# Two attention blocks on one core: exponentials without a shift, a range check with a second program behind a branch, and another split of the PSUM banks

## The chip, the cores and the metric

The kernel runs on one core of a Trainium2 chip. The metric is device time in microseconds (us). TensorE is called PE (its weight loads PEld), ScalarE ACT, VectorE DVE, GpSimd POOL and the engine that issues the DMAs SP. Every run is one of a program on one core.

## The reference, cut to what matters

Two blocks whose outputs stand side by side, each with 2048 rows, width 1024 and 32 heads of width 32.

```python
# A: full attention
scores = einsum('bhqd,bhkd->bhqk', q, k) * Dh ** (-0.5)      # 2048 x 2048 per head
p = softmax(scores); o = einsum('bhqk,bhkd->bhqd', p, v);  out_A = o @ wo
# B: four segments of 512 rows; causal softmax inside one, plus a memory of the earlier ones
p = softmax(logits + mask); a_dot = p @ vs
a_mem = (pq @ M) / (pq @ z + 1e-6);  o = g * a_mem + (1 - g) * a_dot
M = M + pk^T vs;  z = z + sum(pk);   out_B = o @ wo
```

A softmax stays the same if the exponent is shifted by any number per row. Without a shift it is right as long as no exponential overflows and no sum vanishes; with these inputs the scores are small.

## The kernel before: the parts that the change touches

The kernel is a list scheduler in Python. It keeps a model of each engine's time, records instructions in an order that this model likes, and writes that fixed order out with semaphores, so the order is settled before the kernel runs.

```python
SLOTS = [(0, 1, 2), (3, 4)]      # PSUM banks of the two score slots
OLB = 5                          # PV output and row sums
PROJ = [6, 7]                    # "side" work: projections, norms, memory, output projection
RING = 20                        # 512-column places for exponentials in SBUF
...
def emit_scores(self, it, n, banks):          # n = 3 or 2 heads of one item
    for part in range(2):                     # two matmuls of 256 columns a bank;
        for bk, (u, st, h) in zip(banks, todo):      # heads sit on different 32-row groups of PE
            ... mms.append((self.ps[:, bk, off:off + w], lhsT, rhs))
    R.op("PE", f, ..., mode="R")
    ...
    cb = self.cbA[b][:, k:k + 1]              # shift: one column, from norms of Q and K
    R.op("ACT", lambda e: e.activation(self.PT[:, s0:s0 + n, 0:width],
             self.ps[:, banks[0]:banks[0] + n, 0:width], ACTF.Exp, bias=cb, scale=SCALE), ...,
         cost=0.171 + n * width * 0.000833)
...
def a_norm(...):     # squares on DVE, column sums on PE, then maxima, a diagonal and a broadcast
...
# in the scheduler's loop, when PE would idle early on: keep it busy with a dummy matmul
if now < 45 and ... and gap >= 0.3 and bank is not None:      # bank: a free one of PROJ + [OLB]
    R.op("PE", lambda e, bank=bank: e.matmul(self.ps[:, bank, :], self.PT[:, RING - 1, 0:P], ...))
```

PE does three kinds of work in turn: scores (row groups), PV with its row sums (column groups), and side work on the whole array.

## Time and profile before

| kernel before | value |
|---|---|
| median of 4 runs | 1350.14 us (1347.47 to 1351.28) |
| PE, ACT busy | 91%, 89% of the span |
| exponentials of scores | 832 (A) + 160 (B) |
| start to start of two exponentials, back to back (median in the trace) | 1424 ns at 1536 columns, 997 ns at 1024: 143 ns + 0.834 ns a column |

The page of the kernel before: busy time, slices of ACT and of the granted PE clock, the chain that ended last, and the two groups of exponentials. A digit stands for a fortieth of the span, and 9 means 90% or more. The chain is followed back from the last instruction to what released each step; a name with q is an engine's sequencer, and "issue" is time with no wait that the profile shows.

```profile
PE 1232.8 (91%) x16968; PEld 509.2 (38%) x17194; DVE 831.7 (62%) x1391; ACT 1206.6 (89%) x1037; POOL 113.9 (8%) x207
...
ACT  3358989999999999999999999999999999999811
...
PEclk9889999999999998999999999999998999999998
...
ACT 66%; PE 23%; DVE 5%; SPq 2%; DMA 2%; issue 1%; POOL 0%; DVEq 0%
...
L471 ACT ACTIVATE PT<-ps,cbA 128x1024 bf16<-128x1024 f32 (+1 forms) x832 | 1013.1, 1365 | 25.1 <-PE ps L454 24.6
...
L471 ACT ACTIVATE PT<-ps,cbB 128x768 bf16<-128x768 f32 (+3 forms) x160 | 171.4, 1197 | 62.5 <-PE ps L454 61.5
```

ACT is full except for the first four slices and the last three, and it holds 66% of the chain. That looks like one bound. But PE has hardly more room, which its busy share does not tell and the order of its weight loads does. Below is the timeline of the kernel before on PEld (start, us, line, how many, idle time before in brackets):

```profile
604.46 0.12 PEld L454 LDWEIGHTS ps<-QA,KA 32*128 32x128 bf16 x6 [0.42 <-ACT PT L471]
604.78 0.10 PEld L520 LDWEIGHTS ps<-PT,VA 128*32 128x32 bf16 x4 [0.21 <-issue]
...
605.33 0.11 PEld L454 LDWEIGHTS ps<-QA,KA 32*128 32x128 bf16 x4 [0.21 <-ACT PT L471]
605.65 0.33 PEld L594 LDWEIGHTS ps<-xA,WA 128*128 128x128 bf16 x3 [0.21 <-issue]
```

Six score matmuls take 604.78 - 604.46 = 0.32 us to the next kind, and four take the same: the heads of one part run side by side, so two or three concurrent heads cost the same. Of the 0.32 us about 0.11 is the change of kind: the two parts of 256 columns take 0.21, since 512 columns of a projection start every 0.215 us in the same trace. The Trainium skill names a cause ("TensorEngine Tiling (Array Packing)", Tiling Modes, Key Properties: changing the tiling mode drains the engine); the gap of 0.21 us before the first load of the next kind, which the loads within one PV run do not have, agrees. Adding up such runs from 200 to 1200 us left PE some 50 us in 1000. That is my estimate, which no view shows; the windows view has PE busy for 929.5 of these 1000 us, with matmul ends that are modelled.

### The profile page before, as it was taken

The page shows a single profiled execution, that of the slowest core. Times are in us where ns is not written, and L with a number is a line of the kernel's source. Part 1 is how long each engine was busy: PE and PEld are TensorE (multiplying, and loading weights), DVE is VectorE, ACT ScalarE, POOL GpSimd, SP SyncE. Part 2 cuts the span into 40 slices and gives each one's busy share as a digit, 9 for nine tenths or more (in the row PEclk, how much of TensorE's full clock was granted, in tenths as well). Part 3 has the DMA queues.
Part 4 walks back from the last instruction along what each step waited for, and adds up shares of the span by engine and source line. Part 5 has one row for each costly group of instructions (what it writes and reads, how often), then busy time and mean ns, then how long its engine had stood idle before and what let it go on. Part 6 is the DMA issues. An engine that isn't in the chain of part 4 may idle for free.

```text
span 1350.1 us, 37376 instructions
## 1 busy us (share of the span) xinstructions
PE 1232.8 (91%) x16968; PEld 509.2 (38%) x17194; DVE 831.7 (62%) x1391; ACT 1206.6 (89%) x1037; POOL 113.9 (8%) x207
## 2 busy tenths in 40 slices
PE   6788999999999988999899999999998999999996
PEld 3433343333333333333333333333333333333442
DVE  3665456555675567656647754757566675567674
ACT  3358989999999999999999999999999999999811
POOL 1000000100011011101100010111011111011110
PEclk9889999999999998999999999999998999999998
DMA  7325122311211122112211112111210113111111
GB/s 211 63 59 130 25 41 62 74 37 25 64 37 33 21 56 37 29 29 60 49 40 30 33 25 58 31 37 30 49 32 21 37 29 96 44 30 43 53 59 47
DMA packets 195870, 66.39 MB, mean 49 GB/s; under 512 B 187008, under 2 KB 187008, under 8 KB 195712
## 3 DMA queue, kind: packets, MB, share of 16 engines
q1 hardware_dynamic: 195712, 63.99, 20.2%
q8 instruction: 135, 2.21, 0.7%
q14 instruction: 23, 0.19, 0.0%
HBM read 40.90 MB, written 8.39 MB: 37 GB/s over the span
## 4 chain that ended last, share of the span: by engine, by line
ACT 66%; PE 23%; DVE 5%; SPq 2%; DMA 2%; issue 1%; POOL 0%; DVEq 0%
ACT PT L471 65%; PE ps L594 13%; PE ps L454 5%; PE ps L520 5%; DVE OL L540 2%; SPq L335 2%; ACT E L762 1%; DVE OL L530 1%; DMA PKt<-PH 1%; DVE outsb L837 1%; DMA WB<-in_B_wk_dram 0%; DMA out_dram<-outsb 0%; SPq L305 0%; DVE SQB L604 0%; DVE KQB L604 0%
## 5 line engine op out<-in xcount | busy, mean ns | idle before, releaser
L471 ACT ACTIVATE PT<-ps,cbA 128x1024 bf16<-128x1024 f32 (+1 forms) x832 | 1013.1, 1365 | 25.1 <-PE ps L454 24.6
L454 PE MATMUL ps<-QA,KA 32*128 32x256 bf16 x4096 | 328.7, 275 | 32.3 <-ACT PT L471 21.0
L520 PE MATMUL ps<-PT,ones 128*32 128x256 bf16 (+1 forms) x4864 | 315.0, 274 | 0.0
L520 PE MATMUL ps<-PT,VA 128*32 128x256 bf16 x4096 | 274.7, 282 | 1.5 <-DVE OL L530 0.8
L540 DVE RECIPROCAL OL<-OL 128x128 f32<-128x128 f32 x256 | 242.3, 948 | 5.2
L471 ACT ACTIVATE PT<-ps,cbB 128x768 bf16<-128x768 f32 (+3 forms) x160 | 171.4, 1197 | 62.5 <-PE ps L454 61.5
L454 PEld LDWEIGHTS ps<-QA,KA 32*128 32x128 bf16 x4096 | 95.3, 92 | 302.3 <-ACT PT L471 249.9
L594 PE MATMUL ps<-xB,WB 128*128 128x512 bf16 x683 | 187.2, 393 | 23.6 <-issue 13.2
L594 PE MATMUL ps<-xA,WA 128*128 128x512 bf16 x679 | 181.0, 385 | 14.1 <-issue 12.7
L491 POOL TENSOR_SCALAR_AFFINE_SELECT PT<-PT 128x512 bf16<-128x512 bf16 (+2 forms) x143 | 83.8, 601 | 1097.7 <-ACT PT L471 1096.5
L520 PEld LDWEIGHTS ps<-PT,VA 128*32 128x32 bf16 x4096 | 107.9, 95 | 134.3 <-issue 125.7
L530 DVE COPY OL<-ps 128x512 f32<-128x512 f32 x128 | 86.6, 677 | 73.6 <-PE ps L520 73.2
L520 PEld LDWEIGHTS ps<-PT,ones 128*32 128x32 bf16 x4864 | 130.7, 97 | 2.7 <-issue 0.3
L594 PEld LDWEIGHTS ps<-xB,WB 128*128 128x128 bf16 x768 | 62.4, 99 | 97.2 <-issue 45.0
L594 PEld LDWEIGHTS ps<-xA,WA 128*128 128x128 bf16 x768 | 61.5, 98 | 84.8 <-issue 34.7
L788 DVE RECIPROCAL den<-den 128x128 f32<-128x128 f32 x96 | 91.1, 949 | 2.1
L604 DVE CAST KQB<-ps 128x512 bf16<-128x512 f32 x64 | 43.4, 679 | 70.8 <-PE ps L594 70.8
L594 PE MATMUL ps<-WoB,OTB 128*128 128x512 bf16 x237 | 62.5, 391 | 8.8 <-DVE OTB L565 5.9
L837 DVE CAST outsb<-ps 128x512 bf16<-128x512 f32 x64 | 43.2, 678 | 37.9 <-PE ps L594 32.4
L454 PE MATMUL ps<-KQB 32*128 32x256 bf16 (+1 forms) x768 | 58.3, 265 | 6.9 <-ACT PT L471 4.3
L604 DVE CAST VT<-ps 128x512 bf16<-128x512 f32 x32 | 21.8, 681 | 67.3 <-PE ps L594 67.3
L594 PE MATMUL ps<-xA,OTA 128*128 128x512 bf16 x242 | 58.6, 380 | 3.7 <-issue 2.0
(76 smaller groups left out, 677.7 us busy)
## 6 DMA issues: line engine op xcount, KB each, us to landing
WB<-in_B_wk_dram SPq DMA_DIRECT2D x32, 256.0 KB, 2.8
WB<-in_B_wq_dram SPq DMA_DIRECT2D x32, 256.0 KB, 2.9
WB<-in_B_wv_dram SPq DMA_DIRECT2D x32, 256.0 KB, 3.1
out_dram<-outsb SPq DMA_DIRECT2D x32, 256.0 KB, 2.0
WA<-in_A_wqkv_dram SPq DMA_DIRECT2D x24, 256.0 KB, 3.6
OTA<-in_A_x_dram SPq DMA_DIRECT2D x16, 256.0 KB, 5.2
WoB<-in_B_wo_dram SPq DMA_DIRECT2D x1, 2048.0 KB, 9.8
xA<-in_A_wo_dram SPq DMA_DIRECT2D x1, 2048.0 KB, 9.4
```

The lines of the kernel that those rows point to most:

```text
L335: R.dma(lambda e: e.dma_start(dst, src), w=keys, issue=0.5)
L454: ins = e.matmul(o, l, r, start=True, stop=True)
L471: op = R.op("ACT", lambda e: e.activation(self.PT[:, s0:s0 + n, 0:width], self.ps[:, banks[0]:banks[0] + n, 0:width], ACTF.Exp, bias=cb, s ...
L491: mo = R.op("POOL", lambda e, ap=ap, pat=pat: e.affine_select(ap, ap, pattern=pat, compare_op=ALU.is_ge, fill=0.0, base=0, channel_multipl ...
L520: ins = e.matmul(o, l, r, start=start, stop=end, skip_group_check=True)
L530: R.op("DVE", lambda e: e.tensor_copy(self.OL[x][:, :], self.ps[:, OLB, :]), r=[("ps", OLB)], w=[("OL", x)], cost=0.66)
L540: R.op("DVE", lambda e, Lq=Lq: e.reciprocal(Lq, Lq), r=[k], w=[k], cost=0.87)
L594: ins = e.matmul(o, l, rh, start=a, stop=z)
L604: op = self.R.op("DVE", lambda e: e.tensor_copy(dst, self.ps[:, bank, :]), r=[("ps", bank)], w=[dkey], cost=0.66)
L762: ex = R.op("ACT", lambda e: e.activation(self.E[:, k0:k1, :], KQ[:, k0:k1, :], ACTF.Exp), r=[("KQB", b, k) for k in range(k0, k1)], w=["E ...
L788: R.op("DVE", lambda e, cs=cs: e.reciprocal(self.den[:, cs], self.den[:, cs]), r=["den"], w=["den"], cost=0.9)
L837: op = R.op("DVE", lambda e, ns=ns, bank=bank, ob=ob: e.tensor_copy(self.outsb[ob][:, ns], self.ps[:, bank, :]), r=[("ps", bank)], w=[("ou ...
```

## The change

Its intent: (1) no shift, so no norms, and the bias of the exponential becomes the immediate 0.0; (2) three slots of two banks, filled two at a time by one run of eight score matmuls, four concurrent heads; (3) that takes six banks for scores, leaving one for PV and one for side work instead of two; (4) the sums and their reciprocals are checked for range at the end, and a flag sends all engines through a complete second program, with shifts, if they fail. Some constants of the scheduler change as well. The core of the diff, cuts marked:

```diff
-SLOTS = [(0, 1, 2), (3, 4)]
-OLB = 5
-PROJ = [6, 7]
+SLOTS = [(0, 1), (2, 3), (4, 5)]
+OLB = 6
+PROJ = [7]
+GROUP = 2
+SLOPE = 0.55
+STICK = True
...
+        cb, ck = 0.0, []
+        if self.shifted and it.kind == "A":
...
-                  cost=0.171 + n * width * 0.000833)
+                  cost=(0.171 if self.shifted else 0.085) + n * width * 0.000833)
...
+            R.op("DVE", lambda e: e.scalar_tensor_tensor(L, L, 1.0, rec, ALU.mult, ALU.add, accum_out=self.rng[:, u.seq:u.seq + 1]),
...
+        if not self.shifted:
+            return                       # no norms in a_norm, b_prep likewise
...
-                it = b if b.kn < a.kn / 2 + LEAD else a
+                it = b if b.kn < a.kn * SLOPE + LEAD else a
...
+                eng.wait_ge(fast.sem["DVE"], fast.count[flag])
+                reg = eng.alloc_register("redo_" + name.lower())
+                eng.reg_load(reg, self.flag[0:1, 0:1])
+                with eng.If_ne(reg, 0):
+                    fast.wait_all(eng)
+                    slow.play(eng, name)
```

## The prediction

> **What bounds the kernel now.** The page's first part shows ScalarE (ACT) busy 89% and TensorE (PE) 91% of 1350 us. By the windows view, from 200 to 1200 us ACT is busy 988 of 1000 us; PE is nearly full as well: its weight loads, cut into runs of one kind (scores, PV, projections), leave about 50 us of those 1000 free. In the chain of waits ACT's exponentials are 65%. ACT idles mainly outside that stretch: about 68 us before 200 us, 36 us from 1280 us to the last exponential at 1323 us, then 27 us of output projection after it.
>
> **What the change does, costed.**
> - ACT. Back to back, the trace's exponentials start every 1424 ns (1536 columns) and 997 ns (1024), that is 0.834 ns a column + 143 ns. Without a bias pointer the fixed part shrinks: the Trainium skill ("ScalarE: Activation LUTs", What ACT_TABLE_LOAD costs) says an ACTIVATE with immediates takes about 93 ns less than one with a pointer. The trace shows half of this: the 1024-column exponentials of E, with an immediate bias, are followed after 947 ns, 50 ns less. I take 946 ns. But slots of two banks instead of 3+2 mean 1024 instructions for 832 in A, 192 for 160 in B. A: 448x0.997+384x1.424=994 us becomes 1024x0.946=969. B: 163 becomes 155. With E and copies, ACT's pure work goes from about 1190 to 1157 us: only 33 us.
> - PE. Runs of 6 and of 4 score matmuls take the same 0.325 us to the next run (drain of about 0.1 included), so eight should take about 0.33. Score runs go from 964 to 598, all changes of kind on PE from 2254 to 1493 (count of the two programs), at about 0.11 us each beyond the matmuls; about 240 norm matmuls go. I estimate PE demand in the middle 15 to 20% lower: no longer a limit.
> - DVE loses about 113 us of norm work, gains 128 fused reductions of about 0.5 us (64 us): off the path.
> - Start: scores no longer wait for norms; A's exponentials should start near 55 to 60 us, not 77, and idle ACT time in the head fall from 68 to about 50 us.
> - Side bank: a projection on one bank cycles in 2.76 us (seen at 66 to 72 us), on two in about 2.0. In the middle PE fills the hole with scores and PV. In the tail ten half-row projections remain after the last PV: about 28 us, plus output DMA 2 us, flag load and branch (estimate 5), and the last PV: about 40 us after the last exponential, but no late B item with its 32 us hole.
> - A refill needs two of three slots free, so PE has one exponential (0.95 us) to refill: I allow 20 us of ACT stalls in the middle.
>
> Sum: 1157 + 50 + 20 + 40 = 1267 us; I say 1265 us, range 1235 to 1300. Chances: faster by over 2% 0.93, within 2% 0.05, slower 0.02.
>
> **What would show it.** ACT 1024-column period near 946 ns; 1216 exponentials; ACT share rising to about 92% while PE's busy share falls; score runs of eight taking near 0.33 us; last exponential near 1225 us; ten projections spaced 2.7 us at the end; no second pass after the branch.
>
> **What would make it wrong.** Immediate bias not saving anything (then +60 us); four concurrent score matmuls taking longer than two or three, so ACT starves in each refill; the single side bank delaying B's chain so that the exponentials run out of work; a lower granted clock under denser matmuls; the flag triggering the second pass (time doubles).

## The result, and the profile after

The changed kernel took 1257.43 us (median of 4, 1250.86 to 1261.42) against 1350.14 us. The ratio of the fast runs is 0.9311 with a 95% interval of 0.9268 to 0.9354. A ratio is the mean time of one kernel's fast runs over that of the other's fast runs of the same rounds, so it is not quite the ratio of the medians. In a later call the same kernel took 1252.74 us, ratio 0.9276. The prediction was 1265 us, 1235 to 1300.

The page of the changed kernel, lines as before:

```profile
PE 1065.4 (85%) x16720; PEld 492.2 (39%) x16945; DVE 794.4 (63%) x1359; ACT 1134.1 (90%) x1261; POOL 114.3 (9%) x192
...
ACT  3149999999999999999999999999999999999980
...
PEclk8769998999999988989999989889998997999999
...
PE 46%; ACT 40%; DVE 8%; issue 3%; DMA 2%; SPq 1%; DVEq 0%
...
L532 ACT ACTIVATE PT<-ps 128x1024 bf16<-128x1024 f32 (+1 forms) x1216 | 1104.0, 1040 | 43.2 <-PE ps L505 40.0
```

ACT's busy time falls by 72.5 us and PE's by 167 us. ACT stays full in the middle; its low slices at the end are fewer. PE (46%) and ACT (40%) now share the chain. The matmul count (16720 beside 16945 weight loads, where the kernel before shows 16968 beside 17194; a trace can miss a few) shows that the second program did not run. PE's granted clock has more slices below 9, and the first three are 8, 7 and 6. This is a cost that the prediction named only as a risk.

The timeline of the changed kernel: exponentials in a row, and a score run on PEld with what follows it.

```profile
699.16 17.57 ACT L532 ACTIVATE PT<-ps 128x1024 bf16<-128x1024 f32 x19
...
704.03 0.12 PEld L505 LDWEIGHTS ps<-QA,KA 32*128 32x128 bf16 x8 [0.42 <-ACT PT L532]
704.36 0.10 PEld L581 LDWEIGHTS ps<-PT,VA 128*32 128x32 bf16 x4 [0.21 <-issue]
```

Nineteen exponentials take 17.57 us; the median start to start is 904 ns. Eight score matmuls take 0.33 us to the next kind; six took 0.32.

Where ACT's time went. "Pure" is the count of exponentials times the median back-to-back distance of their shape, plus E and copies. E is block B's own exponential for its memory, read as bfloat16 from SBUF with an immediate bias; the copies move transposed inputs out of PSUM. "Late" is the sum, in the trace, of what each start came later than that distance, from 90 us to the last exponential. The prediction meant its 50 us for the head up to 200 us; the trace has 64.6 us there.

| part of the sum | predicted | changed kernel |
|---|---|---|
| pure work of ACT | 1157 us | 1088 x 0.904 + 128 x 0.690 + 34 = 1106 us |
| ACT idle in the first 100 us | 50 us | 63.5 us |
| late exponentials in the middle | 20 us | 49 us |
| after the last exponential | 40 us | 34.9 us |
| sum | 1267 us | 1253 us (profiled span 1254.6) |

The total came out close by luck: a term sized 51 us too high and the tail, 5 us too high, stood against two that were 42 us too low together. The experiments take the terms one by one.

### The profile page after: what moved, and what is told of

Same layout as the page of the kernel before. It is cut to its first block, busy times and chain, and to the rows that moved or that the text cites. A ratio compares the mean times of both kernels' runs of the same rounds, so it can differ in the third digit from the quotient of the medians.

```text
span 1254.6 us, 37128 instructions
## 1 busy us (share of the span) xinstructions
PE 1065.4 (85%) x16720; PEld 492.2 (39%) x16945; DVE 794.4 (63%) x1359; ACT 1134.1 (90%) x1261; POOL 114.3 (9%) x192
## 4 chain that ended last, share of the span: by engine, by line
PE 46%; ACT 40%; DVE 8%; issue 3%; DMA 2%; SPq 1%; DVEq 0%
ACT PT L532 39%; PE ps L674 24%; PE ps L581 12%; PE ps L505 9%; DVE SQ L604 2%; DVE OL L591 1%; DVE outsb L924 1%; DMA out_dram<-outsb 1%; SPq L384 1%; PE ps L423 1%; ACT E L849 1%; DMA WB<-in_B_wv_dram 1%; DVE den L875 1%; ACT xA L428 0%; DVE KA L684 0%
## 5 line engine op out<-in xcount | busy, mean ns | idle before, releaser
L532 ACT ACTIVATE PT<-ps 128x1024 bf16<-128x1024 f32 (+1 forms) x1216 | 1104.0, 1040 | 43.2 <-PE ps L505 40.0
L581 PE MATMUL ps<-PT,ones 128*32 128x256 bf16 (+1 forms) x4864 | 301.5, 279 | 0.0
L581 PE MATMUL ps<-PT,VA 128*32 128x256 bf16 x4096 | 253.8, 279 | 20.1 <-ACT PT L532 15.4
L505 PE MATMUL ps<-QA,KA 32*128 32x256 bf16 x4096 | 212.0, 283 | 43.7 <-ACT PT L532 38.0
L604 DVE RECIPROCAL SQ<-OL 128x128 f32<-128x128 f32 x256 | 242.6, 948 | 4.4
L505 PEld LDWEIGHTS ps<-QA,KA 32*128 32x128 bf16 x4096 | 61.6, 93 | 228.2 <-ACT PT L532 202.6
L552 POOL TENSOR_SCALAR_AFFINE_SELECT PT<-PT 128x512 bf16<-128x512 bf16 x128 | 84.3, 660 | 674.4 <-ACT PT L532 669.5
L581 PE MATMUL ps<-PT,VB 128*32 128x256 bf16 (+1 forms) x768 | 54.5, 296 | 14.4 <-DVE OL L591 10.8
L608 DVE SCALAR_TENSOR_TENSOR OL<-OL,SQ 128x256 f32<-128x256 f32 x128 | 57.8, 451 | 2.5
L684 DVE CAST SQB<-ps 128x512 bf16<-128x512 f32 x32 | 22.0, 689 | 58.8 <-PE ps L674 58.8
```

What stands on the lines that cost most here:

```text
L505: ins = e.matmul(o, l, r, start=True, stop=True)
L532: op = R.op("ACT", lambda e: e.activation(self.PT[:, s0:s0 + n, 0:width], self.ps[:, banks[0]:banks[0] + n, 0:width], ACTF.Exp, bias=cb, s ...
L552: mo = R.op("POOL", lambda e, ap=ap, pat=pat: e.affine_select(ap, ap, pattern=pat, compare_op=ALU.is_ge, fill=0.0, base=0, channel_multipl ...
L581: ins = e.matmul(o, l, r, start=start, stop=end, skip_group_check=True)
L604: R.op("DVE", lambda e, cs=cs: e.reciprocal(rec[:, cs], L[:, cs]), r=[ko], w=[k], cost=0.93)
L608: R.op("DVE", lambda e: e.scalar_tensor_tensor(L, L, 1.0, rec, ALU.mult, ALU.add, accum_out=self.rng[:, u.seq:u.seq + 1]), r=[k, ko], w=[k ...
```

## The experiments

Twelve kernels ran, all with the right result. Where labels begin with a_, the edit is to the changed kernel; with b_, to the kernel before.

### The immediate bias taken back (a_pointer)

```diff
-        cb, ck = 0.0, []
+        cb, ck = self.zcol[:, 0:1], ["zcol"]     # one column of zeros, memset at the start
```

> The changed kernel, but every score exponential takes a zero bias from a one-column tile instead of the immediate 0.0; the order of the instructions on the matmul engine is the same. Theory (the middle is bound by the exponentials and the immediate saved the whole 93 ns of each): the 1024-column period goes from 904 back to 997 ns, 1216 x 0.093 = 113 us more pure work, of which some 30 us vanish in today's stalls: 1330 to 1350 us. Rival (the gain comes from the relief of the matmul engine, the bias is a side matter): at most 40 us more, below 1300 us.

Measured: 1342.07 us (1338.67 to 1347.29), ratio to the kernel before 0.9951 (0.9896 to 1.0006). The median distance of 1024-column exponentials went to 997 ns. Page of this kernel, busy time and chain, and the group of these exponentials:

```profile
PE 1092.9 (82%) x16720; PEld 485.9 (36%) x16945; DVE 803.1 (60%) x1360; ACT 1233.5 (92%) x1261; POOL 113.5 (8%) x192
...
ACT 86%; PE 8%; DVE 2%; SPq 1%; DMA 1%; issue 1%; DVEq 0%
...
L534 ACT ACTIVATE PT<-ps,zcol 128x1024 bf16<-128x1024 f32 x1088 | 1110.8, 1270 | 25.7 <-PE ps L507 25.6
```

This is the theory's number and far from the rival's. With four concurrent matmuls, no norms and the same order on PE, but a bias read from memory, the gain is half a per cent, and the interval does not exclude none. ACT then holds 86% of the chain: PE's relief lies idle. Smaller slots mean 224 more exponentials, each with the fixed part of 143 ns, 32 us of further ACT work (an estimate from these two numbers) against what the other parts free.

### The immediate bias alone, in the kernel before (b_immediate)

```diff
-                                                ACTF.Exp, bias=cb, scale=SCALE),
+                                                ACTF.Exp, bias=0.0, scale=SCALE),
```

> The kernel before, norms and maxima still computed, but the score exponentials take the immediate bias 0.0; the order on the matmul engine is the same. Theory (in the kernel before the matmul engine was as full as the exponentials, about 950 of 1000 us): the exponentials get 992 x 0.093 = 92 us shorter, but only 35 to 55 us show: 1295 to 1315 us. Rival (only the exponentials bounded it): nearly all of it shows, 1255 to 1270 us.

Measured: 1313.62 us (1313.03 to 1314.96), ratio 0.9726 (0.9677 to 0.9774). Page of this kernel:

```profile
PE 1212.1 (92%) x16968; PEld 507.1 (39%) x17194; DVE 828.4 (63%) x1391; ACT 1140.4 (87%) x1037; POOL 114.3 (9%) x207
...
PE 71%; DVE 13%; ACT 8%; issue 3%; DMA 3%; SPq 1%; DVEq 0%
```

Again inside the theory's range. Of 992 x 93 ns = 92 us that ACT no longer needs, 37 us show; the chain has turned from ACT (66% before) to PE (71%). The shortest distances of 1024 columns are 904 ns, as in the changed kernel, but the median is 921: here even exponentials in a row often wait a little. So the two halves of the change are worth 0.5% and 2.7% alone and 7% together. Each uncovers the other's bound. The first "half" is everything but the bias (no norms, slots, banks, order), and STICK and the other rules of the scheduler that changed with it were not run alone, except for the constant of b_slope below.

### One slot at a time (a_group1)

```diff
-GROUP = 2
+GROUP = 1
```

> The changed kernel with its slots filled one at a time, so two concurrent score matmuls and about twice the score runs. Theory (the grouping in fours is what frees the matmul engine): some 600 more runs of 0.33 us each fill it, the middle becomes bound by it, 1330 to 1360 us. Rival (the exponentials bound it either way, and one slot at a time is even refilled more easily): within 15 us of the changed kernel's 1257 us.

Measured: 1378.25 us (1374.78 to 1378.94), ratio 1.02 (1.0147 to 1.0253): 121 us more than the changed kernel, above the theory's range and far from the rival. The windows view of this kernel says how (columns: window in us, its length, busy us of PE, PEld, DVE, ACT, POOL, granted clock, DMA share, GB/s):

```profile
100.00:1240.00 1140.00, 1040.45 (x15591) 451.38 (x15778) 685.06 (x1180) 1071.01 (x1194) 92.87 (x152) 0.99 0.20 42
1240.00:1377.00 137.00, 92.57 (x623) 36.32 (x622) 75.73 (x129) 18.60 (x25) 12.11 (x20) 0.97 0.14 45
```

With 866 score runs in place of 598 the scheduler finds no room on PE for side work and puts it off. In the last 137 us ACT is busy for 18.6 us while projections go one after another through the single side bank. This placement is read from the trace, not tested. The grouping pays by leaving PE room for side work while the exponentials run. The edit also changes the schedule's order, so the size (which I expected at 75 to 100 us) is not a clean price of the extra runs.

### The choice of items alone (b_slope)

```diff
-                it = b if b.kn < a.kn / 2 + LEAD else a
+                it = b if b.kn < a.kn * 0.55 + LEAD else a
```

> The kernel before with only the rule that picks between A and B items changed as in the change (slope 0.55 for 0.5). Theory (the late B item and its 32 us hole near the end go away with this one constant): 20 to 30 us less, 1320 to 1330 us. Rival (the side work only moves elsewhere, since the matmul engine is full anyway): within 8 us of 1350 us.

Measured: 1350.42 us (1347.65 to 1352.43), ratio 1.0005 (0.9953 to 1.0057). My theory fell. The hole of 31.6 us in ACT before the last B item is still there in its trace, up to 1313.7 us. It is there in b_immediate too (31.9 us). In the changed kernel the longest idle time of ACT after 100 us is 2.0 us, and it stays at 2.0 us or less with the pointer bias (a_pointer) and with norms as well (a_norms). So neither the bias nor the missing norms removed the hole; it went with the new slots, banks and order, which I have not separated.

### Flag, branch and second program cut out (a_onepass)

```diff
-            for shifted in (False, True):
+            for shifted in (False,):
...
-                eng.wait_ge(fast.sem["DVE"], fast.count[flag])
-                ... (register load, If_ne, second program)
```

> The changed kernel with the flag, the branch and the second program cut out; the first pass is unchanged. Theory (the branch costs only what the end of the trace shows: about 3.5 us between the landing of the last output and the end, for the taken branch on the matmul and DMA-issuing engines): 1253 to 1255 us. Rival (a program twice as long costs also along the way): 1245 us or less.

Measured: 1247.84 us (1244.53 to 1251.88), ratio 0.9244 (0.9221 to 0.9266). Against the 1257.43 us of the first call this looked like 10 us and fell between the two expectations. Against the changed kernel run again in a later call (1252.74 us, ratio 0.9276) it is 4 to 5 us, no more than the spread between calls. The traces agree with that: from the last exponential to the end 30.3 us, against 34.9 and 33.8. In the changed kernel's trace PE's own branch takes 3.5 us at the end (1250.16 to 1253.66 us). The Trainium skill ("Runtime: NRT & Kernel Launch", Instruction fetch mechanics) says that a taken branch out of the prefetched pages waits for a DMA fetch, which fits a jump over some 17,000 matmuls; no run tests it. The other engines stand still too: after their branches ACT, DVE and SP come to the next instruction 3.3, 3.8 and 3.0 us later, and POOL, with few instructions, after 0.4 us. The rival is not excluded: in the profiled executions the last exponential of a_onepass also ends 6 to 7 us earlier. ACT idles 57.0 us in the first 100 us there, not 63, and PE's clock was at half speed for 23.9 us of the first 90, not 44.4. Since this share also differs between other kernels with the same order on PE (34.1 us in a_pointer), chance may explain it; one profile each cannot tell.

### Only the second program (a_norms)

```diff
-            for shifted in (False, True):
+            for shifted in (True,):          # and no flag, no branch
```

> Only the second program of the changed kernel, run once with no flag and no branch: the new banks, slots and order, but norms, maxima and pointer biases as in the kernel before, so the layout alone. To be compared with the changed kernel with pointer biases, 1342 us, which has no norms. Theory (the norms cost the head some 10 us and load the one side bank): 1350 to 1375 us, no faster than the kernel before. Rival (the norms were hidden): 1335 to 1345 us.

Measured: 1358.31 us (1356.48 to 1359.37), ratio 1.005 (1.0025 to 1.0074). The new banks, slots and order with norms and pointer biases are half a per cent slower than the kernel before. Against a_pointer, which has no norms but has the branch, the norms are worth 16 us, or about 20 us with the branch allowed for. The two programs also differ in the order on PE, because the scheduler's model counts other costs with shifts, so this is not a clean price of the norms. Its first A score starts at 74.6 us, no later than a_pointer's 76.0, so the norms did not cost their time in the head as I had expected. From the first A score to the last exponential it takes 1246.7 us for a_pointer's 1227.1: the time goes there.

### Dummies in the head (a_warm)

The changed kernel has no dummy matmul left. As I read the scheduler, the side bank and the PV bank are both held at the start by work that waits for its loads, so the old rule never finds a free one. The kernel before has seven dummies, as its timeline on PE shows:

```profile
1.51 3.17 PE L992 MATMUL ps<-PT 128*128 128x512 bf16 x7 [1.51 <-DVE PT L389]
```

Windows of the kernel before, then of the changed kernel (the granted clock is the third number from the end):

```profile
30.00:60.00 30.00, 21.66 (x260) 13.26 (x260) 19.61 (x36) 13.60 (x14) 3.95 (x7) 0.96 0.47 100
60.00:100.00 40.00, 35.59 (x299) 13.85 (x302) 23.50 (x44) 18.25 (x16) 2.63 (x4) 0.85 0.26 57
```

```profile
30.00:60.00 30.00, 19.07 (x150) 10.25 (x150) 11.90 (x22) 6.03 (x7) 1.34 (x2) 0.73 0.27 61
60.00:100.00 40.00, 30.75 (x303) 12.99 (x307) 7.14 (x11) 21.43 (x24) 0.00 (x0) 0.72 0.17 37
```

The experiment gives the dummies another home:

```diff
+            free = [s for s in SLOTS if self.slot_end[s] <= now]
+            if now < 100 and gap >= 0.2 and free and self.ready(["den"]) <= now:
+                bank = free[-1][-1]          # a score bank that is not in use
+                R.op("PE", lambda e, bank=bank: e.matmul(self.ps[:, bank, :], self.fill[:, 0:P], self.fill[:, 0:512], ...), cost=MM)
```

> The changed kernel with dummy matmuls into a free score bank wherever the schedule leaves the matmul engine idle for 0.2 us in the first 100 us. Theory (the granted clock was 0.5 in 44 of the first 82 us because the matmul engine idled, and that delayed the first A scores): the clock stays near 1 from about 14 us, A exponentials start 12 to 16 us sooner, 1241 to 1247 us. Rival (the head is bound by loads and by turns on the side bank, not by the clock): within 4 us of 1257 us.

Measured: 1243.62 us (1242.29 to 1245.71), ratio 0.9202 (0.9181 to 0.9223). Windows of this kernel:

```profile
30.00:60.00 30.00, 23.10 (x204) 11.96 (x206) 13.45 (x25) 6.61 (x8) 1.34 (x2) 1.00 0.32 70
60.00:100.00 40.00, 35.19 (x473) 15.92 (x483) 11.06 (x17) 31.66 (x35) 0.00 (x0) 1.00 0.43 113
```

The recorded half-speed time of PE in the first 90 us fell from 44.4 to 6.8 us (the clock records begin at 17.6 and 9.6 us; before them the spacing of the matmuls is that of half speed), the first A score came at 69.3 us instead of 78.7, and ACT's idle time in the first 100 us fell from 63.5 to 52.8 us. From 60 to 100 us ACT is busy for 31.7 us instead of 21.4. The theory holds, for 9 to 14 us according to which call of the changed kernel one compares with; the first A score came 9 us sooner, not 12 to 16.

### The scheduler's costs set to the measured ones (a_calibrated)

```diff
-DRAIN = 0.105
+DRAIN = 0.115
...
-                  cost=(0.171 if self.shifted else 0.085) + n * width * 0.000833)
+                  cost=(0.143 if self.shifted else 0.050) + n * width * 0.000833)
...   (a score run without its 0.02, a PV part 0.003 for 0.02)
```

> The changed kernel with the scheduler's costs set to what the trace shows (exponential 50 ns + columns instead of 85, score run without its 20 ns, PV part 3 ns for 20, change of kind 115 ns for 105). Theory (about 49 us of late exponentials in the middle come partly from a schedule made with wrong durations): 10 to 25 us less, 1232 to 1247 us. Rival (they come from the short refill window and the clock's slow spells, which no cost mends): within 6 us of 1257 us.

Measured: 1255.09 us (1252.66 to 1256.28), ratio 0.9279 (0.9259 to 0.9299): the same as the changed kernel, as the rival said. The last exponential ends 12 us earlier (1207.4 for 1219.7 us), but what follows it takes 47.1 us for 34.9: more projections were left for the one side bank. That made a second experiment worth while (a_tail_cal).

### The changed kernel again (after_again)

> The changed kernel itself once more, so that small differences have a reference of the same call and chip. Both theories: 1250 to 1261 us, ratio 0.926 to 0.935; if it comes out near 1248 us, the 10 us that cutting the branch seemed to save were mostly the spread between calls.

Measured: 1252.74 us (1251.53 to 1253.83), ratio 0.9276 (0.9263 to 0.9288). Calls differ by some 5 us for the same kernel, so smaller differences than that between calls are not read as effects here.

### Dummies all along (a_warmall)

Between 90 and 1200 us of the changed kernel the granted clock falls to 0.5 in 14 spells of 3.4 to 13.7 us, 109 us in all (48 us in the kernel before). In the 3.4 us before each of these spells PE was busy for at most 63% of the time; the median of such stretches is 94%. After exponentials that start in a spell the next are late by 20.6 us in 107 (by 14.0 us if one counts those that start in a spell themselves), elsewhere by 28 us in some 1050. The Trainium skill ("TensorE: Matmul & The Clock Gate", Part 1) says that the clock is halved after an idle window of about 3.4 us. Here no gap on PE was over 1.93 us in the middle, so no long gap was needed. But a thin stretch is no sure sign either. On the 3.4 us grid of the clock records ten more stretches of at most 63% were not followed by a spell at once (355.5 us: 55% busy, next spell at 430.6 us), and in a_group1 four spells followed stretches that were 68 to 80% busy. What starts a spell stays open. The trace's clock is granted at 1.0 or 0.5 only, and the matmuls follow it: eight of a projection take 3.6 us in a spell and 1.9 us outside.

```diff
+            spare = [b for b in PROJ if b not in self.bank_busy and self.bank_end[b] <= now] + [s[-1] for s in free]
+            if now >= 100 and gap >= 0.1 and room >= 0.4 and spare and (scores are left):      # shortened, partly in words
+                four matmuls of ones, 128 columns each, into spare[0]          # on top of a_warm
```

> The changed kernel with dummy matmuls in the first 100 us (1243.6 us) and further dummies, about 240 groups of four 128-column matmuls, wherever its schedule leaves the matmul engine idle later on. Theory (each slow spell of the clock follows a stretch of about 3.4 us in which the matmul engine was under 0.6 busy; about 20 us of late exponentials fall in these spells): slow spells after 90 us shrink from 104 us to under 40, 1226 to 1236 us. Rival (the clock falls for another reason, or dummies get in the way of the refills): 1240 us or more.

Measured: 1228.78 us (1227.18 to 1229.6), ratio 0.9101 (0.9089 to 0.9114), the fastest kernel. Page of this kernel:

```profile
PE 1093.5 (89%) x17738; PEld 539.2 (44%) x17972; DVE 796.5 (65%) x1360; ACT 1130.4 (92%) x1261; POOL 115.7 (9%) x192
...
ACT  3279999999999999999999999999999999999980
...
PEclk8999999999999999999999999999999999999999
```

About 240 groups of useless matmuls take 15 us off a_warm's time. There is no slow spell between 90 and 1200 us any more, and the last exponential ends at 1191.7 instead of 1207.7 us. Of the late exponentials 31 us remain, for 47 in a_warm. The theory holds: it said 1226 to 1236 us. The rest may be what the short refill window costs, or the fixed order, which was not tried further.

### Several banks for the tail (a_tail, a_tail_cal)

The chain of the changed kernel at its end, in order of time (start, us, what):

```profile
1240.50 1.91 PE ps L674 x8
1242.42 0.02 issue
1242.44 0.70 DVE outsb L924
1243.14 0.05 issue
1243.19 1.91 PE ps L674 x8
```

Eight matmuls, an eviction, eight matmuls: 2.69 us a half row, since both use the one bank.

```diff
+            if cur is None and not self.qA and not self.qB and not self.tail:   # all scores are out
+                self.tail = True
+                for s in SLOTS:
+                    for b in s:
+                        self.banks.append(b)
...   (first halves are then evicted by ACT, and PV goes before side work)
```

> The changed kernel with dummies in the first 100 us, and once the last scores are issued the six score banks serve the output projection, whose evictions alternate between the vector and scalar engines. Theory (ten half rows on one bank cost 2.7 us each, on several 1.75): from last exponential to end 25 to 28 us instead of 34, 1233 to 1238 us. Rival (the tail is bound by the last unit's normalisation and the output's landing): 1241 us or more.

Measured: 1235.03 us (1232.24 to 1237.19), ratio 0.9148 (0.9135 to 0.9162). From the last exponential to the end 24.9 us instead of a_warm's 34.2; half rows now come every 1.73 us. The theory holds. The edit changes banks, evictions and the order of PV at once, but the tail of the kernel before, with its two side banks and DVE alone, has the same distance (start, us, what):

```profile
1336.33 0.69 DVE L837 CAST outsb<-ps 128x512 bf16<-128x512 f32 x1 [1.24 <-PE ps L594]
1338.06 0.69 DVE L837 CAST outsb<-ps 128x512 bf16<-128x512 f32 x1 [1.04 <-PE ps L594]
```

So more than one bank is enough for it.

> The same with the scheduler's costs set to the measured durations as well. Theory (the measured costs brought the last exponential 12 us forward but left more projections for the one side bank, so the gain was given back in a tail of 47 us; with several banks it stays): 1224 to 1233 us. Rival (no gain from the costs): as the kernel above, or slower.

Measured: 1239.45 us (1236.08 to 1242.06), ratio 0.9176 (0.9158 to 0.9193). The theory fell. With the costs corrected and the tail widened, the last exponential ends at 1208.8 us, no earlier than a_tail's 1205.5, and the tail is 30.7 us. The 12 us seen in a_calibrated were not carried over; its slow clock spells had also been fewer (72 us for 109), here they are 102 us. So better costs alone brought nothing.

The dummies all along and the wide tail touch different parts of the run. Together they might give about 1220 us, an estimate (1228.8 less the 9 us by which a_tail's tail is shorter); that kernel was not run.

## Why the prediction was right, point by point

- **PE and ACT both near their limits before: right.** The two single-sided experiments show it: relief of PE alone 0.5%, relief of ACT alone 2.7%, both 7%. The weights were off: the prediction saw "only 33 us" less ACT work and put a bias that saves nothing at +60 us; taking the immediate back cost 85 to 89 us.
- **"I take 946 ns" for the exponential: this step was mis-sized.** It measured 904 ns, 42 ns less on 1088 of the 1216 instructions, and 690 ns for the others. The skill's statement ("ScalarE: Activation LUTs", What ACT_TABLE_LOAD costs), about 93 ns for a bias pointer, was exactly what the traces show (997 - 904 = 93). I had set it aside for a sign in the trace, E's exponentials followed after 947 ns. But E reads another memory and another type, and its distance stayed 946 ns after the change. A comparison of two instructions that differ in more than one thing was taken for one.
- **"idle ACT time in the head fall from 68 to about 50 us": failed.** It fell by 3 us, to 64.6 us by 200 us. I had read the exponentials at 77 us as A's; they were B's. The first A score moved only from 83.9 to 78.7 us. Scores no longer wait for norms, but PE's clock was recorded at half speed for 44.4 us of the first 90, for 17.1 before. a_warm brings back 9 us of the start. That the loss of the seven dummies (all before 4.7 us) caused the slow head is not shown: a_warm adds at least 54, from 5 to 83 us.
- **"I allow 20 us of ACT stalls in the middle": mis-sized, 49 us.** Some 14 to 21 us are the slow spells of the clock; a_warmall takes away 16 us in the middle. The prediction named a lower clock under denser matmuls. Here adding matmuls raised it.
- **Eight score matmuls in 0.33 us, 598 score runs, 1493 changes of kind: right**, and a_group1 shows that without this room the side work ends up behind the exponentials. PE's busy time fell by 14%; 15 to 20% less demand in the middle was the estimate.
- **The tail, "about 40 us": 34.9 us**, with the projections spaced 2.69 us as predicted; a_tail and the tail of the kernel before show that the one bank is what spaces them. Flag and branch cost 4 to 5 us, predicted 5. The late B item's hole of 32 us is gone, as predicted, but for a reason that stays open (b_slope).
- **DVE off the path: right.** The fused reduce takes 57.8 us and its accumulator reads 10.4 us, 68 where 64 were estimated; DVE's total still fell by 37 us.

## What to carry to other kernels

When two engines are both nearly full, cost each half of a change against the other engine's limit: either half alone may show almost nothing. When the matmul engine gets room, look at its granted clock: here half-speed time in the middle rose from 48 to 109 us. Cheap dummy matmuls in the schedule's gaps, aimed at any bank that is free, can pay, and a change that takes banks away can leave the old ones without a place, as the scheduler's rule reads here. Before taking a cost from a neighbouring instruction in the trace, check that it differs only in what you want to measure.

## What the Trainium skill lacked or had wrong

- "ScalarE: Activation LUTs": it gives 186 ns + 0.833 ns a column with immediates and an overlap of 93 ns, so 93 ns of fixed cost back to back. Exponentials of 32-bit PSUM scores showed 50 ns with an immediate bias and 143 ns with a pointer; E, from bfloat16 in SBUF, showed 94 ns, as the page has it. The difference of 93 ns for the pointer agrees.
- "TensorE: Matmul & The Clock Gate": Part 1 speaks of idle windows of about 3.4 us and, under "A second HAM failure mode: psum-queue depth-cycling", of frequent short idle times between groups of matmuls, without saying how short or how many. Here stretches of 3.4 us in which PE was 36 to 63% busy, with no gap over 1.93 us, came before all 14 slow spells of the middle, ten like them had no spell after them, and about 240 groups of four short matmuls removed the spells.
- "Runtime: NRT & Kernel Launch": it gives no time for a taken branch to a far target, and neither does another page. Here it is 3.5 us on PE in the changed kernel and 4.5 us in a_warm.
- "TensorEngine Tiling (Array Packing)": it gives no cost of a change of mode; here about 0.11 us beyond the matmuls (0.33 us for a run whose two parts of 256 columns take 0.21).
